# Windowed attention and two feed-forward layers on one core: the planner's order, with offsets for twelve stretches in place of three

## The chip, the core and the metric

The kernel runs on one core of a Trainium2 chip. The metric is the device time of one execution in microseconds (us), the median of several runs. Engine names are those of the profile: PE is TensorE, DVE VectorE, ACT ScalarE, POOL GpSimd, SP the engine that only issues transfers; PEld is the loading of PE's weights.

## What is computed

```python
# q, k, v: (4, 8, 576, 64); heads 0-3 see a window of 32 keys, heads 4-7 every 4th key of 128
scores = scale * np.matmul(q, k.transpose(0, 1, 3, 2))
attn = softmax(np.where(masks, scores, -1e9))
x = np.matmul(attn, v)                      # as (2304, 512)
h = x @ w_in                                # (512, 2048)
x = (h * np.cos(h)) @ w_out                 # (2048, 512)
gate = 1.0 / (1.0 + np.exp(-(x @ w_gate)))  # (512, 1536)
out = (gate * (x @ w_val)) @ w_out2         # (1536, 512)
```

## The kernel before, in words

The 2304 tokens are cut into 6 chunks of 384. Every matrix product of the two layers is made of three PE products, because each operand is split into a high and a low part (`mm3`, lines 896 to 898: high by low, low by high, high by high).

**Attention.** It runs in 24 pairs (12 groups of 192 tokens, plain and dilated heads), two groups to a chunk. For each pair there is `load_qk` (lines 619 and 626), `load_v` (685, 689, 696), a transpose on PE (`transp`, 705), copies out of it (`q_out` and `k_out`, 723 and 727), `scores` on PE (740), the maximum on DVE (`s_max`, 752), the exponential on ACT (`s_exp`, 759), `s_eps` and `s_rec` on DVE (762, 765), `s_norm` on POOL (769), another transpose (`p_transp`, 774), a copy (`p_out`), the product with v (`pv`, 793), and the split of the result into `x_hi` (ACT, 810) and `x_u` or `x` (DVE, 814).

**First layer.** It has 96 steps (chunk and block of 128 hidden columns): all six chunks with blocks 0 to 7, then all six with blocks 8 to 15. Step n has 12 products `h` into one of two PSUM banks `ps_h`, then a chain that alternates ACT and DVE: `turn` (946), `part` (950), `cos` (953), `g` (956, it frees the bank), `g_hi` (963, or on DVE 961), `g_lo` (966). Its end allows the 12 products `x2` into `acc`. The attention of the next chunks is woven between the steps.

**Weights.** They come from memory as 512 KB pieces. Each goes through `w_load` (SP, lines 480 and 483, two buffers `raw`), `w_low` and `w_mag` (ACT, 487 and 492), `w_shift` and `w_rnd` (DVE, 496 and 503; `w_rnd` gives the `raw` buffer back, so the load after the next one can start), `w_hi` (ACT 510 or DVE 508) and the low part `w` (POOL, 514). The weights of the second layer are prepared while the first one runs: sums of blocks on DVE (`w_sum`, 564), high parts on ACT (`w_bhi`, 572), low parts `w_blo` (576; the function `lo` of `block_tasks` takes the engine as an argument), then a transfer to memory (`w2_save`, 581). There are 18 such blocks of four low parts each; blocks 12 to 17 belong to the last product.

**Second layer.** Three sections (pairs of chunks) of 12 steps with 42 products (1203 to 1205), each followed by sums on DVE (1221, 1232), sigmoids on ACT (1229, 1236) and products on DVE (1239); between them and behind them the products with the last weights (`o`, 1351 to 1353, whose operands `o_hi` and `o_lo` make, 1326 and 1330), fed by loads `ow` (1337).

**What sets the order.** No engine chooses at run time. Class `Plan` holds every piece of work as a task with an engine, a duration, the tasks it depends on, buffers it takes and gives, and a number `prio`. `Plan.run` (line 112 on) goes through the run in its own reckoning of time; whenever an engine falls free, it takes the ready task with the lowest `prio`. `Plan.emit` then writes each engine's instructions in that order, the transfers of SP too. An engine works through its instructions strictly in this order, so an instruction that has to wait holds up all behind it. The `prio` of a task of the first layer is the number of its step, of a task that feeds one the number of the step that it is for, less a lead; the chain of a step has its number less `URGENT` (20). The second layer starts at 96 and each of its steps adds 2.75. To this `Plan.add` (line 132) adds an offset by kind of task, from one of three tables: `NUDGE` for `prio` under 16, `NUDGE_MID` under 44, `NUDGE_LATE` from there on (20, 23 and 18 entries, none larger than 9.25).

`MOVES` (line 61) is a list that `emit` applies after the planning: the four low parts `w_blo` of block 16 and the four of block 17 are taken out of POOL's order and put into DVE's, ahead of the tasks named.

**Filler.** While `cold()` holds (until step 7 has begun), `keep_warm` (line 1466) lets PE do bfloat16 products on an identity matrix whenever the plan has nothing else for it. Their results are not used.

Of the kernel before, what the change touches and what calls it, by code (L numbers as in the profile page):

```python
# [46 lines left out]
QK_LEAD, V_LEAD = 3.2, 3.6  # L47
A_LEAD, EXP_LEAD = 2.1875, 0.5
COLD, DENSE = 1.25, 1.0
NUDGE_UNTIL, NUDGE_FROM = 16, 44  # L50
NUDGE = {"k_out": -1.25, "load_qk": -0.25, "load_v": 1.25, "p_out": -7, "p_transp": 0.5, "pv": -3.5, "q_out": -1.25,
         "s_eps": 4.75, "s_exp": 1, "s_max": 2, "s_move": -1.25, "s_norm": -8, "scores": -4, "w": -5.75, "w_mag": -2.5,
         "w_rnd": 0.25, "w_top": -2.5, "x_hi": -6, "x_save": -4.5, "x_u": -5}
NUDGE_MID = {"head": -5.5, "k_out": 4, "load_v": -1.5, "p_out": -0.75, "p_transp": -4.25, "pv": -2.25, "q_out": -2.5,
             "s_eps": 5, "s_exp": -4.25, "s_max": -5.5, "s_norm": 1.5, "s_rec": -5, "scores": -2.25, "transp": -5.25, "w_hi": 3.25,
             "w_load": -1, "w_mag": 7.5, "w_rnd": 2.25, "w_shift": 1, "w_top": 4.25, "x": 0.5, "x_hi": -4.75, "x_u": 5.25}
NUDGE_LATE = {"o_lo": -5.75, "o_sum": 6, "ow": 3, "w2": -4.75, "w2_save": 1.75, "w_blo": -0.5, "w_load": 2.25,
              "w_low": -2.5, "w_mag": 1, "w_rnd": 0.5, "w_sum": 2.5, "w_top": 3.5, "x2_load": -2.25, "x2_take": -0.25, "x_again":
              5.75, "xs": 9.25, "xs_hi": 5.5, "xs_sum": -2}
MOVES = [(("w_blo", 16, 0), "dve", ("g", 92)), (("w_blo", 16, 1), "dve", ("g", 92)), (("w_blo", 16, 2), "dve",  # L60
         ("part", 93)), (("w_blo", 16, 3), "dve", ("part", 93)), (("w_blo", 17, 0), "dve", ("x2_take", 11, 0)), (("w_blo", 17,
         1), "dve", ("x2_take", 11, 0)), (("w_blo", 17, 2), "dve", ("x2_take", 11, 0)), (("w_blo", 17, 3), "dve", ("x2_take",
         11, 0))]
WARM, WARM_NS = 1200, 57


class Plan:
# [28 lines left out]
    def add(self, key, eng, dur, fn, deps=(), prio=0.0, take=(), give=(), table=None, port=False, lat=None, step=None,  # L96
            after=(), gate=None, alt=None, other=None, dma=0):
        assert key not in self.tasks, key
        if key[0] != "warm":
            prio += (NUDGE if prio < NUDGE_UNTIL else NUDGE_MID if prio < NUDGE_FROM else NUDGE_LATE).get(key[0], 0.0)  # L100
        self.tasks[key] = dict(key=key, eng=eng, dur=dur, fn=fn, deps=deps, prio=prio, take=take, give=give, table=table,
                               port=port, lat=lat or 0, step=step, after=after, gate=gate, alt=alt, other=other, dma=dma)

# [135 lines left out]
    def emit(self, todo):  # L239

        at = {k: i for i, (k, e, fn) in enumerate(todo)}
        eng = {k: e for k, e, fn in todo}
        queue = {e: [k for k, x, fn in todo if x == e] for e in ("pe", "act", "dve", "pool", "sp")}
        for k, e, ahead in MOVES:
            queue[eng[k]].remove(k)
            eng[k] = e
            queue[e].insert(queue[e].index(ahead), k)
        count, then, free = {}, {}, dict(self.room)
        for k, t in self.tasks.items():
            ds = set(t["deps"]) | set(t["after"])  # L250
            count[k] = len(ds)
            for d in ds:
                then.setdefault(d, []).append(k)
        for q in queue.values():
            for a, b in zip(q, q[1:]):
                then.setdefault(a, []).append(b)
                count[b] += 1
        self.progress = None
        ready, held = [at[k] for k in at if not count[k]], []
        heapq.heapify(ready)  # L260
        left = len(todo)
        while ready:
            i = heapq.heappop(ready)
            k, e, fn = todo[i]
            t = self.tasks[k]
            if any(free[g] < t["take"].count(g) for g in t["take"]):
                held.append(i)
                continue
            if eng[k] != e:
                fn = t["fn"] if eng[k] == t["eng"] else (t["alt"] or t["other"])[2]  # L270
            for g in t["take"]:
                free[g] -= 1
            if t["step"] is not None:
                self.progress = t["step"]
# [12 lines left out]
        assert not left, "the moves leave no order"
# [3 lines left out]
def windowed_attention_mlp_kernel(ctx, tc, q, k, v, w_in, w_out, w_gate, w_val, w_out2, out):  # L291
# [164 lines left out]
    def w_tasks(i):  # L456
# [63 lines left out]
        else:  # L520
            gate = need - 8 if kind == "out2" else min(W_GATE[2] + j * W_GATE[3], need - 8)
        add(("w_load", i), "sp", 550, load, [], pr - 2 if i >= 2 * FIRST[0] else max(NEG_GS * (i / 4 - 6) + W_START, pos(-A_LEAD - 1) - QK_LEAD + 0.1), take=["raw"], dma=1900, gate=gate,
            after=[("w_load", w_order[w_order.index(i) - 1])] if i else [])
        add(("w_low", i), "act", 520, low, [("w_load", i)], pr)

        def keep():
# [991 lines left out]
```

## Time and profile before

| | |
|---|---|
| time, median of 3 runs | 911.76 us (911.38 to 912.44) |
| span of the profiled execution, first to last instruction | 910.6 us |
| PE busy | 901.8 us, 99% |
| DVE, ACT, POOL busy | 670.4, 502.1, 173.7 us |
| chain that ended last | PE 88%, DMA 5%, ACT 3%, DVE 2% |
| bytes moved | 225.66 MB, 248 GB/s on the mean |

The span is of one execution; the time of a run adds what lies before the first and behind the last instruction. Busy time counts a stretch once in which several products overlap: a 384 column product is listed with some 335 ns, but the next one starts some 171 ns after it (146 of them fill 25 us). "idle before" of a group is the time in which its engine stood still just before it, with what ended that.

### The profile page before, as it was taken

To read this page: it belongs to the slowest core of one execution; us is meant where nothing else is said; L and a number is where in the kernel's file an instruction comes from. 1 tells how busy PE (TensorE), PEld (TensorE's weight loads), DVE (VectorE), ACT (ScalarE), POOL (GpSimd) and SP (SyncE) were. 2 spreads that over 40 slices of the span, in tenths; PEclk is the share of its full clock that TensorE was granted. 3 is DMA by queue.
4 is the path that set the end of the run, shared out by engine and by line. 5 is a ranking of instruction groups with operands and counts; after the bars stand their busy time and mean duration, and the time that the engine had idled before them with its cause. 6 is when DMAs were issued, how large, how long until landed. Compare 5 with 4: busy or idle time off the path is not lost.

```text
span 910.6 us, 19170 instructions
## 1 busy us (share of the span) xinstructions
PE 901.8 (99%) x6898; PEld 883.8 (97%) x6898; DVE 670.4 (74%) x1656; ACT 502.1 (55%) x1216; POOL 173.7 (19%) x200
## 2 busy tenths in 40 slices
PE   8999999999999999999999999999999999999998
PEld 7899999999999999999999999999999999999998
DVE  6987878877768978757899665786566776566583
ACT  5898889878867656655667312252333343332261
POOL 4535232222236443331230000000000000000000
PEclk9999999999999999999999999999999999999999
DMA  8976856754366899975987798877888997887593
GB/s 205 256 209 200 241 150 207 234 166 129 114 205 259 295 371 340 313 248 181 342 252 287 248 345 269 297 244 250 265 275 274 325 304 242 268 268 216 191 329 98
DMA packets 153039, 225.66 MB, mean 248 GB/s; under 512 B 41968, under 2 KB 117488, under 8 KB 151920
## 3 DMA queue, kind: packets, MB, share of 16 engines
q1 hardware_dynamic: 152144, 224.24, 76.1%
q8 instruction: 55, 0.90, 0.4%
q14 instruction: 40, 0.33, 0.1%
q10 hardware_dynamic: 800, 0.20, 0.1%
HBM read 168.82 MB, written 55.57 MB: 246 GB/s over the span
## 4 chain that ended last, share of the span: by engine, by line
PE 88%; DMA 5%; ACT 3%; DVE 2%; issue 1%; POOL 1%; SPq 0%; POOLq 0%; ACTq 0%; DVEq 0%
PE ps_h L896 7%; PE acc L896 7%; PE acc L898 7%; PE acc L897 7%; PE ps_h L898 7%; PE ps_h L897 7%; PE ps_y L1203 4%; PE ps_y L1204 4%; PE ps_y L1205 4%; PE xy L1351 3%; PE xy L1353 3%; PE xy L1352 3%; PE ps_x L1203 3%; PE ps_x L1205 3%; PE ps_x L1204 3%; PE ps_z L1203 2%
## 5 line engine op out<-in xcount | busy, mean ns | idle before, releaser
L576 POOL TENSOR_TENSOR lr<-lf,lr 128x512 fp32r<-128x512 f32 x64 | 82.1, 1299 | 137.6 <-ACT lr L572 135.9
L896 PE MATMUL acc<-gs,arena 128*128 128x384 f32 x240 | 83.3, 347 | 0.0
L898 PE MATMUL acc<-gs,arena 128*128 128x384 f32 x240 | 80.6, 336 | 0.0
L897 PE MATMUL acc<-gs,arena 128*128 128x384 f32 x240 | 80.4, 335 | 0.0
L946 ACT ACTIVATE r<-ps_h 128x384 int32<-128x384 f32 x96 | 46.9, 488 | 50.2 <-PE ps_h L898 50.0
L1203 PE MATMUL ps_y<-arena 128*128 128x384 f32 x216 | 72.9, 338 | 0.6 <-DVE u L1221 0.3
L1205 PE MATMUL ps_y<-arena 128*128 128x384 f32 x216 | 72.3, 335 | 0.0
L1204 PE MATMUL ps_y<-arena 128*128 128x384 f32 x216 | 72.3, 335 | 0.0
L896 PE MATMUL ps_h<-arena 128*128 128x384 f32 x192 | 68.4, 356 | 1.7 <-DVE arena L814 1.6
L956 DVE TENSOR_TENSOR u<-ps_h,u 128x384 f32<-128x384 f32 x96 | 52.8, 553 | 22.5 <-ACT u L953 22.1
L966 DVE TENSOR_TENSOR gs<-u,gs 128x384 fp32r<-128x384 f32 x96 | 60.9, 634 | 11.3 <-ACT gs L963 10.9
L950 DVE SCALAR_TENSOR_TENSOR u<-ps_h,r 128x384 f32<-128x384 f32 x96 | 52.9, 551 | 19.5 <-ACT r L946 18.8
L953 ACT ACTIVATE u<-u 128x384 f32<-128x384 f32 x96 | 49.8, 522 | 30.2 <-DVE u L950 29.5
L1236 ACT ACTIVATE sg<-sg 128x384 f32<-128x384 f32 x36 | 18.9, 526 | 85.4 <-DVE sg L1232 85.4
L898 PE MATMUL ps_h<-arena 128*128 128x384 f32 x192 | 64.6, 336 | 0.0
L898 PE MATMUL ps_h<-arena,wb 128*128 128x384 f32 x192 | 64.6, 336 | 0.0
L897 PE MATMUL ps_h<-arena,wb 128*128 128x384 f32 x192 | 64.5, 336 | 0.0
L896 PE MATMUL ps_h<-arena,wb 128*128 128x384 f32 x192 | 64.5, 336 | 0.0
L897 PE MATMUL ps_h<-arena 128*128 128x384 f32 x192 | 64.4, 336 | 0.0
L759 ACT ACTIVATE s<-s,mx 128x80 f32<-128x80 f32 (+1 forms) x168 | 59.2, 356 | 0.1
L1326 ACT ACTIVATE arena<-ub 128x384 fp32r<-128x384 f32 x62 | 30.9, 520 | 38.0 <-PE xy L1353 26.0
L492 ACT ACTIVATE wc<-wst 128x512 f32<-128x512 f32 x68 | 45.0, 663 | 7.5 <-DMA wst<-in_moe_w_in_dram 3.3
(225 smaller groups left out, 2887.7 us busy)
## 6 DMA issues: line engine op xcount, KB each, us to landing
arena<-wd SPq DMA_DIRECT2D x108, 512.0 KB, 4.7
lr<-od SPq DMA_DIRECT2D x42, 512.0 KB, 4.7
wd<-lr SPq DMA_DIRECT2D x36, 512.0 KB, 5.0
wst<-in_moe_w_out_dram SPq DMA_DIRECT2D x28, 512.0 KB, 5.3
arena<-od SPq DMA_DIRECT2D x21, 512.0 KB, 6.0
arena<-wd SPq DMA_DIRECT2D x36, 256.0 KB, 3.9
od<-lr SPq DMA_DIRECT2D x18, 512.0 KB, 4.7
wst<-in_moe_w_in_dram SPq DMA_DIRECT2D x16, 512.0 KB, 4.8
```

The source lines that it names most:

```text
L576: on.tensor_tensor(out=l, in0=x, in1=h.bitcast(F32), op=ALU.subtract)
L759: ACT.activation(out=s, in_=s, func=AF.Exp, scale=-1.0, bias=row("mx", u)[:, i:i + 1], accum_out=row("rs", u)[:, i:i + 1])
L896: PE.matmul(ps, wh, xl, start=first, stop=False)
L897: PE.matmul(ps, wl, xh, start=False, stop=False)
L898: PE.matmul(ps, wh, xh, start=False, stop=last)
L950: DVE.scalar_tensor_tensor(st["u"], st["h"], INV_2PI, st["r"], op0=ALU.mult, op1=ALU.subtract)
L953: ACT.activation(out=st["u"], in_=st["u"], func=AF.Sin, scale=TWO_PI, bias=HALF_PI)
L956: DVE.tensor_tensor(out=st["u"], in0=st["h"], in1=st["u"], op=ALU.mult)
L966: DVE.tensor_tensor(out=st["gs"][:, 1, :], in0=st["u"], in1=st["gs"][:, 0, :].bitcast(F32), op=ALU.subtract)
L1203: PE.matmul(st[to], wh, xl, start=first, stop=False, **more)
L1204: PE.matmul(st[to], wl, xh, start=False, stop=False, **more)
L1205: PE.matmul(st[to], wh, xh, start=False, stop=kk == 1, **more)
```

## The change

The three tables become one, `NUDGES`, of twelve tables with 289 entries. A task takes the first whose bound lies above its `prio`: 4, 9, 16, 30, 44, 60, 80, 96, 116, 140, 165, or no bound. The values run from -53 to 90.75, and many more kinds have one, the chain of a step among them (`turn`, `part`, `cos`, `g`, `g_hi`, `g_lo`). Because the chain's `prio` is 20 under its step, the first table holds for the chains of steps 0 to 23, the fourth for steps 36 to 49. `MOVES` is gone, and with it the two places in `emit` that applied it, so all 72 low parts `w_blo` are on POOL. No task is added or taken away, no size, buffer or transfer changes. Nine of the twelve tables are cut here.

```diff
-NUDGE_UNTIL, NUDGE_FROM = 16, 44
-NUDGE = {"k_out": -1.25, "load_qk": -0.25, "load_v": 1.25, "p_out": -7, "p_transp": 0.5, "pv": -3.5, "q_out": -1.25,
-         "s_eps": 4.75, "s_exp": 1, "s_max": 2, "s_move": -1.25, "s_norm": -8, "scores": -4, "w": -5.75, "w_mag": -2.5,
-         "w_rnd": 0.25, "w_top": -2.5, "x_hi": -6, "x_save": -4.5, "x_u": -5}
...
-MOVES = [(("w_blo", 16, 0), "dve", ("g", 92)), (("w_blo", 16, 1), "dve", ("g", 92)), (("w_blo", 16, 2), "dve",
-         ("part", 93)), (("w_blo", 16, 3), "dve", ("part", 93)), (("w_blo", 17, 0), "dve", ("x2_take", 11, 0)), (("w_blo", 17,
-         1), "dve", ("x2_take", 11, 0)), (("w_blo", 17, 2), "dve", ("x2_take", 11, 0)), (("w_blo", 17, 3), "dve", ("x2_take",
-         11, 0))]
+NUDGE_UNTIL = 16
+NUDGES = (
+    (4, {"cos": 11, "g": 2.5, "g_hi": 14.5, "g_lo": -14.5, "head": -7.5, "k_out": -0.75, "load_qk": -0.25,
+         "load_v": 30.75, "p_out": -2.75, "p_transp": -1.75, "part": 2.5, "pv": -1.5, "s_eps": 42.5,
+         "s_exp": 1.25, "s_norm": -28, "s_rec": 3, "scores": -2, "transp": 0.25, "turn": -3.5, "w": -1.25,
+         "w_load": 1.5, "w_low": 0.25, "w_mag": -2.5, "w_rnd": 34.5, "w_shift": -0.5, "x": 0.25, "x2": 0.5,
+         "x_hi": -15.75, "x_save": -4}),
...
+    (30, {"cos": 41, "g": 18.5, "g_hi": 10.5, "g_lo": -2, "head": 5, "load_qk": 1, "load_v": 0.5,
+          "p_out": -3.75, "p_transp": 2.5, "part": -4, "q_out": -2.75, "s_eps": 9.5, "s_exp": 1, "s_max": 15,
+          "s_norm": -4.5, "s_rec": -2.25, "scores": -53, "transp": -0.5, "turn": 2.5, "w_keep": 8.75,
+          "w_load": -5, "w_low": -10.5, "w_mag": -6.75, "x2": -0.5, "x2_save": 1.25, "x2_take": -2.75,
+          "x_hi": 2, "x_save": -5.75, "x_u": -8.75}),
...
+    (96, {"gate_b": -1.5, "h": -45.25, "keep": 1.5, "mul": 1.75, "sig_a": -6, "sig_b": 9, "u2": -17.5,
+          "u3": -3, "va": 6.75, "vb": 21, "w2": 1, "w2_save": 0.5, "w_again": -4.75, "w_bhi": -4.75,
+          "w_blo": 10, "w_load": 2.25, "w_low": 1.75, "w_mag": 4.5, "w_rnd": 37.5, "w_sum": 32, "x2": 2.75,
+          "x2_load": 0.25, "x2_save": -9, "x2_take": -6, "x_again": 5, "xs": 9.25, "xs_hi": -9,
+          "xs_load": -0.5, "xs_sum": 12.25}),
...
+)
@@
-            prio += (NUDGE if prio < NUDGE_UNTIL else NUDGE_MID if prio < NUDGE_FROM else NUDGE_LATE).get(key[0], 0.0)
+            prio += next(d for end, d in NUDGES if prio < end).get(key[0], 0.0)
@@
-        for k, e, ahead in MOVES:
-            queue[eng[k]].remove(k)
-            eng[k] = e
-            queue[e].insert(queue[e].index(ahead), k)
@@
-            if eng[k] != e:
-                fn = t["fn"] if eng[k] == t["eng"] else (t["alt"] or t["other"])[2]
```

## Rows read from the trace of the kernel before

**Rows 1.** The page, busy time, share of the span and instructions of each engine:

```profile
PE 901.8 (99%) x6898; PEld 883.8 (97%) x6898; DVE 670.4 (74%) x1656; ACT 502.1 (55%) x1216; POOL 173.7 (19%) x200
```

**Rows 2.** Busy time of PE by stretch of the span (PEclk: granted clock):

```profile
core 0: us, PE busy (x), PEclk, DMA share, GB/s
0.00:100.00 100.00, 95.23 (x1220) 1.00 0.82 217
100.00:250.00 150.00, 149.64 (x1550) 1.00 0.59 175
250.00:525.00 275.00, 275.00 (x1586) 1.00 0.80 279
525.00:605.00 80.00, 79.43 (x471) 1.00 0.86 293
605.00:870.00 265.00, 265.00 (x1771) 1.00 0.81 262
870.00:911.00 41.00, 37.45 (x310) 1.00 0.61 196
```

**Rows 3.** The last product of all, PE in order of time:

```profile
907.21 0.28 PE L1353 MATMUL zz<-arena 128*128 128x256 f32 x1
```

**Rows 4.** The filler of line 1466 alone, by stretch: PE, PEld, clock, DMA:

```profile
0.00:4.60 4.60, 2.97 (x28) 2.91 (x28) 1.00 0.56 126
4.60:33.00 28.40, 11.53 (x161) 10.14 (x159) 1.00 1.00 232
33.00:54.00 21.00, 2.68 (x36) 2.24 (x36) 1.00 0.99 268
54.00:75.00 21.00, 1.34 (x21) 1.24 (x21) 1.00 0.62 170
```

**Rows 5.** The page's groups, first and third product of a set of three:

```profile
L896 PE MATMUL acc<-gs,arena 128*128 128x384 f32 x240 | 83.3, 347 | 0.0
L898 PE MATMUL acc<-gs,arena 128*128 128x384 f32 x240 | 80.6, 336 | 0.0
...
L896 PE MATMUL ps_h<-arena 128*128 128x384 f32 x192 | 68.4, 356 | 1.7 <-DVE arena L814 1.6
...
L898 PE MATMUL ps_h<-arena 128*128 128x384 f32 x192 | 64.6, 336 | 0.0
```

**Rows 6.** PE in order of time: the first product of a step:

```profile
32.98 0.44 PE L896 MATMUL ps_h<-arena 128*128 128x384 f32 x1 [0.42 <-DVE arena L814]
```

**Rows 7.** The same stretches, all engines: PE, PEld, DVE, ACT, POOL, clock, DMA:

```profile
4.60:33.00 28.40, 26.54 (x463) 23.85 (x461) 22.49 (x118) 21.21 (x83) 12.14 (x20) 1.00 1.00 232
33.00:54.00 21.00, 19.79 (x229) 18.38 (x230) 18.46 (x66) 17.91 (x54) 10.29 (x15) 1.00 0.99 268
```

**Rows 8.** Line 896 alone, one of its groups: min/median/max ns, first and last start:

```profile
L896 PE MATMUL acc<-gs,arena x240: 334/334/445, 53.3 to 511.3; 128*128 128x384 f32 x120
```

**Rows 9.** The low parts of line 576, by engine: min/median/max ns, first and last start:

```profile
L576 POOL TENSOR_TENSOR lr<-lf,lr x64: 725/1300/1842, 261.6 to 480.5; 128x512 fp32r<-128x512 f32 x48, 128x256 fp32r<-128x256 f32 x16
L576 DVE TENSOR_TENSOR lr<-lf,lr x8: 415/682/689, 488.3 to 508.5; 128x512 fp32r<-128x512 f32 x6, 128x256 fp32r<-128x256 f32 x2
```

**Rows 10.** Block 17 in order of time: high parts (ACT), low parts (DVE):

```profile
499.88 0.62 ACT L572 ACTIVATE lr<-lf 128x512 fp32r<-128x512 f32 x1
...
503.18 0.42 ACT L572 ACTIVATE lr<-lf 128x256 fp32r<-128x256 f32 x1
...
506.73 2.22 DVE L576 TENSOR_TENSOR lr<-lf,lr 128x512 fp32r<-128x512 f32 x4
```

**Rows 11.** All engines around blocks 16 and 17 (columns as in rows 7):

```profile
475.00:500.00 25.00, 25.00 (x146) 25.00 (x145) 23.52 (x52) 16.90 (x37) 2.00 (x2) 1.00 0.78 290
500.00:525.00 25.00, 25.00 (x146) 25.00 (x145) 15.42 (x31) 8.28 (x15) 0.00 (x0) 1.00 0.75 251
```

**Rows 12.** Two like DVE subtractions, beside POOL's work and after it: min/median/max ns:

```profile
L966 DVE TENSOR_TENSOR gs<-u,gs x96: 543/557/1594, 47.0 to 506.3; 128x384 fp32r<-128x384 f32 x96
...
L1330 DVE TENSOR_TENSOR arena<-ub,arena x62: 544/550/561, 534.0 to 896.2; 128x384 fp32r<-128x384 f32 x62
```

**Rows 13.** SP's waits between 0 and 80 us (us in total, times, longest):

```profile
SPq L483 <- DVE wc L503: 7.6, 4, 3.6
...
SPq L480 <- DVE wc L503: 3.9, 3, 2.6
```

**Rows 14.** DVE, groups of one tile shape: ns of a copy out of a transpose:

```profile
L727 DVE COPY pt<-psa 96x384 f32<-96x384 f32 x16 | 8.4, 546 | 1.6 <-PE psa L774 1.4
```

More of the change, by code (lines that the diff above doesn't have):

```diff
@@ L49 @@
 COLD, DENSE = 1.25, 1.0
-NUDGE_UNTIL, NUDGE_FROM = 16, 44
-NUDGE = {"k_out": -1.25, "load_qk": -0.25, "load_v": 1.25, "p_out": -7, "p_transp": 0.5, "pv": -3.5, "q_out": -1.25,
-         "s_eps": 4.75, "s_exp": 1, "s_max": 2, "s_move": -1.25, "s_norm": -8, "scores": -4, "w": -5.75, "w_mag": -2.5,
-         "w_rnd": 0.25, "w_top": -2.5, "x_hi": -6, "x_save": -4.5, "x_u": -5}
-NUDGE_MID = {"head": -5.5, "k_out": 4, "load_v": -1.5, "p_out": -0.75, "p_transp": -4.25, "pv": -2.25, "q_out": -2.5,
-             "s_eps": 5, "s_exp": -4.25, "s_max": -5.5, "s_norm": 1.5, "s_rec": -5, "scores": -2.25, "transp": -5.25, "w_hi": 3.25,
-             "w_load": -1, "w_mag": 7.5, "w_rnd": 2.25, "w_shift": 1, "w_top": 4.25, "x": 0.5, "x_hi": -4.75, "x_u": 5.25}
@@ L57 @@
-NUDGE_LATE = {"o_lo": -5.75, "o_sum": 6, "ow": 3, "w2": -4.75, "w2_save": 1.75, "w_blo": -0.5, "w_load": 2.25,
-              "w_low": -2.5, "w_mag": 1, "w_rnd": 0.5, "w_sum": 2.5, "w_top": 3.5, "x2_load": -2.25, "x2_take": -0.25, "x_again":
-              5.75, "xs": 9.25, "xs_hi": 5.5, "xs_sum": -2}
-MOVES = [(("w_blo", 16, 0), "dve", ("g", 92)), (("w_blo", 16, 1), "dve", ("g", 92)), (("w_blo", 16, 2), "dve",
-         ("part", 93)), (("w_blo", 16, 3), "dve", ("part", 93)), (("w_blo", 17, 0), "dve", ("x2_take", 11, 0)), (("w_blo", 17,
-         1), "dve", ("x2_take", 11, 0)), (("w_blo", 17, 2), "dve", ("x2_take", 11, 0)), (("w_blo", 17, 3), "dve", ("x2_take",
-         11, 0))]
+NUDGE_UNTIL = 16
@@ new lines @@
+NUDGES = (
[4 more added lines that the diff above has]
+         "x_hi": -15.75, "x_save": -4}),
+    (9, {"cos": -15.25, "g": 5.25, "g_hi": -9, "g_lo": 2, "head": 4.75, "k_out": -4.75, "load_qk": -4.75,
+         "load_v": -11, "p_out": -5.5, "p_transp": -2, "part": 0.25, "pv": -25, "q_out": -3.25,
+         "s_eps": -10.75, "s_exp": 0.75, "s_norm": 8.25, "s_rec": -1, "scores": -5.25, "transp": -4.75,
+         "turn": -7.5, "x2": -0.75, "x_hi": -1.25}),
+    (16, {"cos": -12, "g": 0.5, "g_hi": -4, "g_lo": -2.75, "h": 0.75, "head": -4.25, "k_out": 4, "load_qk": 1,
+          "load_v": 2, "p_transp": -24.75, "q_out": 1, "s_eps": 5.5, "s_exp": -10.5, "s_max": -2, "s_norm": -7,
+          "s_rec": 2, "scores": -0.75, "transp": -2, "turn": -2.75, "x2_save": -7, "x2_take": -2,
+          "x_hi": -21.5, "x_save": -7, "x_u": -11.5}),
+    (30, {"cos": 41, "g": 18.5, "g_hi": 10.5, "g_lo": -2, "head": 5, "load_qk": 1, "load_v": 0.5,
[3 more added lines that the diff above has]
+          "x_hi": 2, "x_save": -5.75, "x_u": -8.75}),
+    (44, {"g": 3.25, "g_lo": 17.5, "head": -3.75, "k_out": 6.75, "load_qk": -11.5, "load_v": -0.5, "p_out": -1,
+          "p_transp": 15.75, "part": 8.75, "pv": -6, "s_eps": 0.5, "s_exp": 0.5, "s_max": -4.5, "s_norm": 7.25,
+          "s_rec": 7.75, "scores": 5.5, "transp": 5.25, "turn": 3.75, "w": 6, "w_hi": -4, "w_load": -10.5,
+          "w_low": -2.5, "w_mag": -4.5, "w_rnd": -12.5, "w_shift": 1.5, "x": 0.25, "x2": 90.75, "x_hi": -8}),
+    (60, {"cos": -6.25, "g": -22.75, "g_lo": -0.25, "part": 20.75, "turn": 5.25, "w": 7, "w_hi": 18.5,
+          "w_load": -3.25, "w_low": 18.25, "w_mag": -8.25, "w_rnd": 0.25, "w_shift": 1.5, "x2": 0.25,
+          "x2_save": 4.5}),
+    (80, {"cos": 3, "g": 6, "g_hi": 8.25, "g_lo": -24, "gate_b": 8, "h": -0.25, "keep": 1.5, "mul": -6.75,
+          "part": 3, "sig_a": 17.25, "sig_b": -1.5, "turn": 6.75, "u2": 7, "u3": -2, "va": -9.75,
+          "w2_save": -4.75, "w_bhi": 15, "w_blo": -19.75, "w_load": -6, "w_rnd": -7.75, "w_shift": -24.5,
+          "w_sum": 0.5, "x2_load": 9.75, "x2_save": -1, "x2_take": 3}),
+    (96, {"gate_b": -1.5, "h": -45.25, "keep": 1.5, "mul": 1.75, "sig_a": -6, "sig_b": 9, "u2": -17.5,
[3 more added lines that the diff above has]
+          "xs_load": -0.5, "xs_sum": 12.25}),
+    (116, {"gate_b": -12.75, "keep": 6, "o_sum": -5.25, "p": -8.75, "sig_a": 2, "u2": 10.5, "u3": 4, "vb": -2,
+           "w2": 2, "w_again": 4, "w_bhi": -6.25, "w_blo": 2.75, "w_load": -3.25, "w_low": 7.75, "w_mag": 3.5,
+           "w_rnd": -2, "w_sum": -15, "x2_save": 6, "x2_take": -4.75, "xw_load": 1.25, "xw_sum": 7}),
+    (140, {"gate_b": 2.75, "keep": 5, "o": 3, "o_A0": 5, "o_hi": -2, "o_keep": -3, "o_lo": -17.25,
+           "o_save": 19.25, "o_sum": -0.5, "o_u2": -27.5, "ow": 7, "sig_a": -4.5, "sig_b": 2.75, "u2": -4,
+           "u3": -14.5, "va": 1, "vb": -17.25, "w2": 2, "w_bhi": 3, "w_load": 9.5, "w_low": 25.25, "w_rnd": 1,
+           "w_shift": 1.25, "w_sum": 33.5, "xs": 11, "xs_hi": 1}),
+    (165, {"gate_b": -1, "keep": -18.5, "mul": 3, "o": -7, "o_A1": 14.25, "o_B0": 5.25, "o_B1": -4.75,
+           "o_hi": 9, "o_lo": 0.25, "o_save": -11.75, "o_sum": -7.5, "o_u3": -24.25, "ow": -8.75, "p": -8,
+           "sig_a": -9, "sig_b": 7, "u2": 5.5, "u3": 11.5, "va": 1, "vb": -16.5, "w2": 38, "xs": 31.5,
+           "xs_hi": 11, "xw_load": 0.75, "xw_sum": -0.75}),
+    (float("inf"), {"gate_b": 1, "keep": 2, "mul": -19.25, "o": -0.75, "o_A0": -5, "o_B0": 5.5, "o_B1": -4,
+                    "o_hi": -8.25, "o_lo": 18.5, "o_save": 2.75, "o_sum": 18, "o_u2": 17.75, "p": -6,
+                    "sig_a": 4.5, "sig_b": 3, "va": 7.5, "w2": 4.5}),
+)
```

## The prediction

> **What bounds the kernel now.** I read the busy times first. PE is busy for 901.8 of 910.6 us and no other engine comes near it [rows 1]. A busy PE may still do nothing of use, so the second question is where it stands idle or does filler. The stretches answer the first half: between 250 and 525 us, and again between 605 and 870 us, PE is busy in every microsecond (275.00 of 275.00, 265.00 of 265.00), between 525 and 605 us it loses 0.57 us, between 100 and 250 us 0.36 us [rows 2]. What is idle lies in the first 100 us (100 less 95.23 = 4.8 us) and in the end, where 910.6 less the start of the last product at 907.21 is 3.4 us of copying and storing [rows 2, 3]. The filler answers the second half: 2.97 + 11.53 + 2.68 + 1.34 = 18.5 us, all before 75 us [rows 4]. The third loss is inside the busy time. The first product of a set that follows other work is listed longer than its neighbours: 347 against 336 ns in one group and 356 against 336 in another, so (11 x 240 + 20 x 192) ns = 6.5 us over the run go into restarting PE after a turn to attention or after a wait [rows 5].
>
> So everything that an order can give back is some 4.8 + 18.5 us in the start, 6.5 us in turns, and about 1 us behind that. The rest is products, which the change does not touch. Wherever PE is full now, an earlier or later job of DVE, ACT, POOL or SP costs nothing until it makes PE wait. The granted clock is 1.00 in each stretch, which is the level of 2.4 GHz; nothing is to be gained there [rows 2].
>
> **The change, part by part.** The sum is made against the span of 910.6 us; the median run of 911.8 us lies 1.2 us above it, and I carry these 1.2 us along.
>
> *The start (the first three tables).* Of the 23.3 us lost, the stretch up to 4.6 us waits for the first loads and the identity matrix; its 1.63 us of idle (4.60 less 2.97) and 2.97 us of filler are out of reach, since no reordering makes bytes land sooner than the first one asked for [rows 4]. Up to 33 us there is no product of a step, because the first one waits for the split of the attention result of chunk 0 (0.42 us before it at 32.98) [rows 6]. In these 28.4 us PE has 11.53 us of filler and 1.9 us of idle, DVE has 5.9 us free and ACT 7.2 us [rows 4, 7]. From 33 to 54 us filler and idle are 2.68 + 1.2 us, with DVE at 18.46 and ACT at 17.91 of 21 us [rows 4, 7]. The table for `prio` under 4 now says: exponentials' sums (`s_eps`) and rounding of weights (`w_rnd`) behind everything else on DVE, `load_v` behind the weights on SP, `x_hi` and `s_norm` first. That favours the copies and maxima which feed PE, and that is the way in which the first step could come earlier. If all of DVE's 5.9 us were put to use, the first step would come 5.9 us earlier, and the 3.9 us up to 54 us might go as well: 9.8 us is the upper bound. The lower bound is a loss (the second rival). What limits it is the row on transfers: the DMA share is 1.00 and 0.99 up to 54 us [rows 4], so no byte is moved sooner unless another is moved later. I take 3 us, half of DVE's free time before the first step, nearer to the full queues than to the free engine. **-3.0 us.**
>
> *Turns (tables three to five).* Scores, transposes and products with v are ranked anew against `h` and `x2`; `scores` at -53 goes first whenever it is ready. If attention's pieces come in larger groups, PE turns less often. At 6.5 us in all and some 110 ns for one, 445 against 334 ns at the most [rows 8], there are about 60 turns; saving one in eight gives 0.8 us. The bounds are 2 us either way, a third of the rows' sum. **-0.8 us.**
>
> *The late stretches (tables six to twelve).* PE loses 0.57 us from 525 to 605 us and nothing up to 870 us [rows 2]. Whatever else is moved there, `w_sum` by +32, `w_rnd` by +37.5, `u2`, `vb` and the `o` tasks, is covered by the two `ps_h` banks: a bank is free again long before PE is back at it. If that cover went, each wait would cost its length and a restart. I take half of what is lost, bounded by 0.6 us of gain and 2 us of loss. **-0.3 us.**
>
> *The eight low parts.* On DVE they take 6 x 682 + 2 x 415 ns = 4.9 us at the most; on POOL eight take 6 x 1300 + 2 x 725 ns = 9.3 us [rows 9]. On the path lies block 17, the last one, since its `w2_save` and the load `ow` behind it stand ahead of the first `o` products on SP. Its high parts are done on ACT between 500.5 and 503.6 us, but DVE comes to the low parts only at 506.73 and ends at 508.95 [rows 10]. POOL, which does nothing from 482 us on [rows 9, 11], could start at 500.5 and need 3 x 1300 + 725 ns = 4.6 us, so it would be done at about 505.1, earlier than DVE. Block 16 is made and saved ahead of block 17 either way and is not on this path. DVE gets 4.9 us back in a stretch where it is busy for 23.52 + 15.42 of 50 us, and PE waits for nothing there [rows 11]. **0 us**, with bounds of 0.5 us either way.
>
> There is something that speaks against it. DVE's subtraction at line 966, made while POOL works, takes 557 ns in the median but up to 1594; the same shape at line 1330, after POOL's last instruction, never exceeds 561 [rows 12]. So POOL's work holds DVE up now and then. The Trainium skill, page "SBUF — State Buffer", section "SBUF: two separate sides", says why: VectorE and GpSimd share one pair of ports, and whichever starts first keeps it for its whole instruction while the other is blocked. The trace agrees in kind. By that rule alone the eight parts hold DVE for up to 9.3 us.
>
> By the rows, DVE gives up 4.9 us and may be held for 9.3, a net 4.4 us at the worst, against 1.5 + 9.6 us that it has free in these two stretches; so the term stays at 0 [rows 11].
>
> Sum: 911.8 - 3.0 - 0.8 - 0.3 + 0 = **907.7 us**.
>
> **The rivals.**
> *It only changes places.* In the start the transfers set the pace: share 1.00 and 0.99 up to 54 us [rows 4]. Then a different rank of the same jobs moves filler from one stretch to another, and the rest of the run is full anyway [rows 2]. Offsets also do nothing where only one job is ready. For it: the DMA share, and DVE and ACT at 85 to 88% after 33 us. Against it: 11.5 us of filler before 33 us with both engines free for a fifth of it [rows 4, 7]. Time: 911.8 less the turns' 0.8, 911 us. That includes the case that the change does not do what it says.
>
> *Weights come late (slower).* Place: `w_rnd` on DVE in the first 75 us. It is what gives the `raw` buffer back, and SP's loads of weights already wait for it seven times, for 7.6 + 3.9 = 11.5 us [rows 13]. With +34.5 it stands behind every other ready job on DVE. Behind a waiting load on SP stand the loads of q, k and v, and behind a late weight `h` and `x2`. One job more in front of each rounding is 546 ns [rows 14]; twelve of the sixteen first weights are loaded after the first four, so 12 x 0.55 = 6.6 us. It decides from the point at which a weight of the first eight steps lands later than PE gets to it: after 54 us there is only 1.34 us of filler to absorb that [rows 4]. Time: 911.8 + 6.6 - 1.3 = 917 us. For it: a DVE with 88% busy rarely gets to its last job. Against it: 2.5 us of 21 are still free there [rows 7], and a rank behind only counts while something else is ready.
>
> *DVE held by POOL, or a bank late (slower).* The chain of steps 36 to 49 has `cos` at +41, behind all other work of ACT, and the eight parts hold DVE. Each would need to use up the slack of a bank. If three or four steps lost 1 us each, 915 us. For it speaks only the maximum of 1594 ns [rows 12]; against it that PE lost 0.36 us in 150 with the same cover [rows 2].
>
> **How the numbers follow.** A measurement of this kernel tells 0.2% (1.8 us) from no change. Forecast (start and turns give 2 to 10 us): 0.58. Changes places: 0.18. Weights late: 0.16, DVE held or a bank late: 0.08. So faster 0.58, same 0.18, slower 0.24. The range reaches from most of the start's bound, 911.8 - 9.8 = 902, to just under the price of late weights, 916.5: outside lie a tenth below and a tenth above. The likeliest case alone is 903 to 910.
>
> **What would show it.** Right: fewer than 244 fillers, the last before 71 us; the first step product before 33 us, by about the gain; line 576 on POOL alone, 72 times, with block 17 saved no later than now; no new PE wait after 250 us. Weights late: the waits of lines 480 and 483 for line 503 grow past 11.5 us, and filler grows between 33 and 75 us. DVE held: line 966 or 950 with a longer mean, and PE waits between 200 and 525 us. The forecast is wrong if the filler stays near 18.5 us and the time still moves by over 2 us, for then the gain or loss came from a place I call full.

## The result, and the profile after

The changed kernel takes 917.49 us in the median of six runs (915.92 to 918.55), the kernel before 911.57 us in six runs beside them. The ratio is 1.0051, with a 95% interval from 1.0036 to 1.0066: slower by 0.5%, about 4.7 us. Ratio and interval are taken over all of these runs, so the ratio need not be the quotient of the two medians. The prediction of 907.7 us had the wrong sign, and the result lies above its range. The profiled execution has a span of 915.2 us (before 910.6) and a run time 1.8 us above that.

In the changed kernel every source line below the tables stands 31 lines further down: line 927 is line 896 of before, 997 is 966, 607 is 576. The page's busy times, against [rows 1]:

```profile
PE 902.5 (99%) x6877; PEld 883.7 (97%) x6877; DVE 668.3 (73%) x1632; ACT 510.5 (56%) x1234; POOL 183.4 (20%) x208
```

The engines do nearly the work that they did: POOL has 9.7 us more, for its eight parts, ACT 8.4 us more, DVE 2.1 us less. The loss is in waits, and busy time by stretch, set against [rows 2], says where (PE busy, then granted clock, DMA share and GB/s):

```profile
0.00:100.00 100.00, 94.72 (x1178) 1.00 0.85 222
...
200.00:250.00 50.00, 48.98 (x509) 1.00 0.47 137
250.00:450.00 200.00, 197.58 (x1185) 1.00 0.78 277
450.00:525.00 75.00, 75.00 (x432) 1.00 0.79 278
525.00:605.00 80.00, 79.56 (x472) 1.00 0.83 280
605.00:870.00 265.00, 264.56 (x1752) 1.00 0.80 260
```

From 250 to 450 us, where PE had been busy without a gap, it now stands idle for 2.42 us, from 200 to 250 us for 1.02 us and from 605 to 870 us for 0.44 us. Between 200 and 870 us that makes 4.32 us idle, where the kernel before has the 0.57 us of 525 to 605 us and no more. Each stop adds a restart of some 0.1 us that counts as busy [rows 8]. With the 3.75 us of idle time that are new, that is most of the 4.6 us by which the span grew. The first 100 us are no better than before: 5.28 us idle in place of 4.77.

PE's waits between 200 and 300 us, and between 440 and 450 us, name what came late (us in total, times, longest):

```profile
PE ps_h L927 <- DVE u L987: 1.5, 2, 1.0
PE acc L927 <- DVE o L1061: 0.2, 1, 0.2
...
PE acc L927 <- DVE gs L997: 1.6, 1, 1.6
```

The longest one is the easiest to follow. First DVE, then POOL, then PE in order of time:

```profile
440.70 0.42 DVE L527 TENSOR_SCALAR wc<-wc 128x512 int32<-128x512 int32 x1
441.04 0.35 DVE L992 CAST gs<-u 128x384 fp32r<-128x384 f32 x1
441.31 1.52 DVE L595 TENSOR_TENSOR lf<-lf 128x256 f32<-128x256 f32 x1
442.75 1.61 DVE L997 TENSOR_TENSOR gs<-u,gs 128x384 fp32r<-128x384 f32 x1
444.28 0.68 DVE L534 CUSTOM_DVE_ANT_0 lf<-wst,wc 128x1024 uint16<-128x1024 uint16 x1
...
441.12 2.82 POOL L607 TENSOR_TENSOR lr<-lf,lr 128x512 fp32r<-128x512 f32 x2 [5.18 <-ACT lr L603]
...
444.41 0.44 PE L927 MATMUL acc<-gs,arena 128*128 128x384 f32 x1 [1.61 <-DVE gs L997]
```

The sum on line 595 takes 1.52 us where its median is 0.42, and the subtraction `g_lo(78)` on line 997 takes 1.61 us where its median is 0.56, while POOL's two low parts of block 13 run beside them for 2.82 us. PE has finished `x2(77)` and stands still until `g_lo(78)` is there. In the kernel before, `g_lo(78)` came right behind `g(79)` on DVE. In the new order eight jobs stand between them: the shift and the rounding of weight 59, three sums of block 13, the shift of weight 60, `g_hi(78)`, which was on ACT, and `w_sum(13,3)`. What was there 4.9 us early in the old order (the rows are below, where the prediction is answered) is now late when POOL holds DVE: the two holds make up (1.52 - 0.42) + (1.61 - 0.56) = 2.2 us, the wait is 1.6 us.

In the same way `h(43)` waits at 280.95 us for 0.46 us, behind a shift of 1.52 us and a `g_lo` of 1.19 us, and `x2(40,3)` waits at 287.69 us for 0.23 us behind a cast of 1.42 us and a sum of 1.50 us. The wait at 219.28 us has another cause: `cos(30)` stands on ACT behind `w_mag(25)`, whose weight was late from memory. ACT in order of time:

```profile
217.56 0.66 ACT L523 ACTIVATE wc<-wst 128x512 f32<-128x512 f32 x1 [2.09 <-DMA wst<-in_moe_w_in_dram]
218.13 0.51 ACT L984 ACTIVATE u<-u 128x384 f32<-128x384 f32 x1
```

### The profile page after: what moved, and what is told of

Its sections match the earlier page's. It is cut to its first block, busy times and chain, and to the rows that moved or that the text cites. A ratio compares the mean times of both kernels' runs of the same rounds, so it can differ in the third digit from the quotient of the medians.

```text
span 915.2 us, 19166 instructions
## 1 busy us (share of the span) xinstructions
PE 902.5 (99%) x6877; PEld 883.7 (97%) x6877; DVE 668.3 (73%) x1632; ACT 510.5 (56%) x1234; POOL 183.4 (20%) x208
## 4 chain that ended last, share of the span: by engine, by line
PE 50%; DVE 1%; DMA 1%; SPq 0%; issue 0%; ACT 0%; DVEq 0%
PE ps_y L1234 4%; PE ps_y L1236 4%; PE ps_y L1235 4%; PE xy L1382 3%; PE xy L1384 3%; PE xy L1383 3%; PE ps_x L1234 3%; PE ps_x L1236 3%; PE ps_x L1235 3%; PE ps_z L1234 3%; PE ps_z L1235 3%; PE ps_z L1236 3%; PE zz L1382 1%; PE zz L1384 1%; PE zz L1383 1%; PE acc L927 1%
## 5 line engine op out<-in xcount | busy, mean ns | idle before, releaser
L607 POOL TENSOR_TENSOR lr<-lf,lr 128x512 fp32r<-128x512 f32 (+1 forms) x72 | 91.7, 1293 | 139.5 <-ACT lr L603 112.1
L997 DVE TENSOR_TENSOR gs<-u,gs 128x384 fp32r<-128x384 f32 x96 | 64.2, 670 | 15.1 <-ACT gs L994 14.2
```

Of the source, the lines that this page charges most:

```text
L607: on.tensor_tensor(out=l, in0=x, in1=h.bitcast(F32), op=ALU.subtract)
L997: DVE.tensor_tensor(out=st["gs"][:, 1, :], in0=st["u"], in1=st["gs"][:, 0, :].bitcast(F32), op=ALU.subtract)
```

## The experiments

An edit of the form `(job, engine, next)` puts that job ahead of the job `next` on that engine; where `MOVES` is added to the changed kernel, the two places in `emit` that apply it are back too (not printed). "Ratio" is to the kernel before on the same chip, with its 95% interval.

**The eight parts alone.** The kernel before without its moves, so that only the low parts of blocks 16 and 17 go to GpSimd:

```diff
-MOVES = [(("w_blo", 16, 0), "dve", ("g", 92)), (("w_blo", 16, 1), "dve", ("g", 92)), (("w_blo", 16, 2), "dve",
...
```

> The kernel before with the eight low parts of blocks 16 and 17 back on POOL and nothing else changed. Theory (the loss of the changed kernel comes from a few places between 200 and 450 us where the new order puts a step's chain behind work that is held up): no change, 911.6 us within 0.6, and no new PE wait between 480 and 530 us. Rival (the eight parts themselves cost it, by holding DVE or by a later save of block 17): 914.5 us or more, with a PE wait behind 488 us.

Measured: 914.17 us, ratio 1.0022 (1.0014 to 1.0031), 2.0 us slower. PE has a new wait, and the trace shows the hold in front of it (waits, DVE, POOL):

```profile
PE ps_y L1193 <- DVE u L946: 1.3, 1, 1.3
...
501.90 1.66 DVE L1077 TENSOR_TENSOR arena<-xt,arena 128x384 fp32r<-128x384 f32 x1
503.48 1.43 DVE L951 CAST gs<-u 128x384 fp32r<-128x384 f32 x1
504.83 0.54 DVE L946 TENSOR_TENSOR u<-ps_h,u 128x384 f32<-128x384 f32 x1
...
501.77 4.27 POOL L566 TENSOR_TENSOR lr<-lf,lr 128x512 fp32r<-128x512 f32 x3 [7.29 <-ACT lr L562]
```

Three of block 17's parts hold a subtraction and a cast, and `g(95)` comes 1.3 us late. So the theory written before this run, no change, was wrong: the parts are not free in the old order.

**The start alone.** The changed kernel with its first three tables, the old ones behind them (written here by their old names) and the old moves:

```diff
-    (30, {"cos": 41, "g": 18.5, "g_hi": 10.5, "g_lo": -2, "head": 5, "load_qk": 1, "load_v": 0.5,
...
+    (44, NUDGE_MID),
+    (float("inf"), NUDGE_LATE),
 )
+MOVES = [(("w_blo", 16, 0), "dve", ("g", 92)), (("w_blo", 16, 1), "dve", ("g", 92)), (("w_blo", 16, 2), "dve",
...
```

> The first three of the new tables (prio under 16), then the old middle and late tables and the old list of moves. Theory: the start is a wash, 911.6 us within 1.2; PE has done as much useful work by 200 us as before. Rival (late weights in the first 75 us, a loss that is carried on): 914 us or more, filler over 18.5 us. My forecast on record would have it at 908.6.

Measured: 913.11 us, ratio 1.0001 (0.9991 to 1.0012). In its profile the first product of a step starts at 32.22 us, 0.76 us before [rows 6], and the filler is 14.20 + 2.53 = 16.7 us in place of 18.5 [rows 4]. The time does not show it: the start is worth nothing that can be measured.

**The later tables alone.** The changed kernel with the old first table, up to `prio` 16 and written here by its old name, in the place of its first three; the eight parts stay on GpSimd:

```diff
 NUDGES = (
-    (4, {"cos": 11, "g": 2.5, "g_hi": 14.5, "g_lo": -14.5, "head": -7.5, "k_out": -0.75, "load_qk": -0.25,
...
+    (16, NUDGE),
     (30, {"cos": 41, "g": 18.5, "g_hi": 10.5, "g_lo": -2, "head": 5, "load_qk": 1, "load_v": 0.5,
```

> The old first table up to prio 16, then the nine new tables from there on; no moves. Theory: the loss is made by these tables, so 914 to 918 us, with PE waits of 0.4 to 2 us in a few places between 200 and 450 us (not at the same steps, since the start is another one). Rival (late weights in the start): 912.5 us or less.

Measured: 920.55 us, ratio 1.0090 (1.0076 to 1.0104). The same wait for a `g_lo` (1.6 us) stands in its profile, and three for a `g` (2.7 us in all, the longest 1.8 us near 304 us). The tables from `prio` 16 on make the loss by themselves. They lose more than the whole change does and more than was expected, so the parts of the change do not simply add up.

**No GpSimd at 442 us.** The two low parts that run there go to VectorE, behind `g_lo(78)`:

```diff
+MOVES = [(("w_blo", 13, 0), "dve", ("w_rnd", 60)), (("w_blo", 13, 1), "dve", ("w_rnd", 60))]
```

> The changed kernel with two low parts of block 13 put on DVE behind the last piece (g_lo) of step 78's chain, so that POOL does nothing while DVE makes the sum and g_lo at 441 to 444 us. DVE's order in front of g_lo stays. Theory (POOL holds DVE: the sum took 1.52 us in place of 0.42 and g_lo 1.61 in place of 0.55): the sum and g_lo take 0.42 and 0.55 us, PE's wait of 1.61 us before the x2 products of step 78 goes, span 1.7 us (1.3 to 2.1) under 915.2. Rival (g_lo is simply too far back in DVE's order): the wait stays over 1 us and the span within 0.6 of 915.2.

Measured: 916.5 us, ratio 1.0042 (1.0028 to 1.0055). With POOL silent the sum and `g_lo(78)` have their usual length again, and PE's wait of 1.61 us is gone. But the edit carries its own cost, 1.28 us of DVE ahead of `part(80)`, and PE then waits 0.76 us for `g(80)`, which frees the bank of the next `h`. The profiled span is 915.1 us, so the 1.7 us did not come back (DVE in order of time, then PE's waits):

```profile
441.87 0.42 DVE L605 TENSOR_TENSOR lf<-lf 128x256 f32<-128x256 f32 x1
442.20 0.55 DVE L1007 TENSOR_TENSOR gs<-u,gs 128x384 fp32r<-128x384 f32 x1
442.68 1.28 DVE L617 TENSOR_TENSOR lr<-lf,lr 128x512 fp32r<-128x512 f32 x2
...
PE ps_h L937 <- DVE u L997: 0.8, 1, 0.8
```

**`cos(30)` ahead of the late weight.**

```diff
+MOVES = [(("cos", 30), "act", ("w_mag", 25))]
```

> The kernel after, with one job moved on ACT: cos(30) stands ahead of w_mag(25), whose load came late at 217 us. Theory (the in-order queue of ACT makes cos(30) and so h(32) late): PE's wait of 1.02 us at 219 us is gone, its restart too, and nothing else waits in its place, so 917.5 - 1.2 = 916.3 us. Rival (the weight itself is late for its own step, and the wait only moves on): PE waits about 1 us a little later, time 917.5 us.

Measured: 915.63 us, ratio 1.0033 (1.0020 to 1.0046). `w_mag(25)` still waits 1.9 us for its weight, but behind `cos(30)`, and PE's wait of 1.02 us at 219 us is gone. One of 0.39 us stands at 220 us in its place: a transpose waits for a copy on ACT behind the same late weight. The interval does not part this run from the changed kernel; the trace shows that the wait for `g(30)` comes from ACT's queue.

**`w_sum` behind `g_lo`.** The order of two DVE jobs, POOL left as it is:

```diff
+MOVES = [(("w_sum", 13, 3), "dve", ("w_rnd", 60))]
```

> The kernel after, with one job moved on DVE: w_sum(13,3) stands behind g_lo(78), not ahead of it. GpSimd's two low parts of block 13 stay where they are. Theory (GpSimd's instruction at 441.1 us holds whichever DVE instruction comes next until it ends): g_lo(78) (line 997) now takes 1.2 to 1.6 us in the place of w_sum, ends near 442.8 us, and PE's wait of 1.61 us falls to 0.3 to 0.6. Rival (only the order of the queue counts, and the long durations are not held by GpSimd): g_lo(78) takes 0.55 us, ends near 441.9 us and PE does not wait at all. Time by either 917.5 less 1.1 to 1.7, 916.1 us; it is the row of line 997 that tells them apart.

Measured: 917.49 us, ratio 1.0047 (1.0028 to 1.0065), no gain. Its row of `g_lo(78)` is what the theory expected, and the sum behind it is held as well:

```profile
441.57 1.53 DVE L1006 TENSOR_TENSOR gs<-u,gs 128x384 fp32r<-128x384 f32 x1
443.02 1.50 DVE L604 TENSOR_TENSOR lf<-lf 128x256 f32<-128x256 f32 x1
444.45 0.68 DVE L543 CUSTOM_DVE_ANT_0 lf<-wst,wc 128x1024 uint16<-128x1024 uint16 x1
```

So it is not the job that is long, it is whatever stands there. PE waits 0.2 us for `g_lo(78)` and then 1.3 us for `g(80)`, which now comes late. Neither theory had the second wait.

**Four places at once.**

```diff
+MOVES = [(("cos", 30), "act", ("w_mag", 25)), (("w_sum", 13, 3), "dve", ("w_rnd", 60)),
+         (("w_shift", 34), "dve", ("g_lo", 40)), (("g_lo", 40), "dve", ("x2_take", 4, 1)),
+         (("x2_take", 4, 3), "dve", ("w_sum", 0, 3)), (("w_sum", 0, 3), "dve", ("part", 43))]
```

> The kernel after, with six jobs moved in four places and everything else left: cos(30) ahead of w_mag(25) on ACT (219 us); on DVE w_sum(13,3) behind g_lo(78) (444 us), w_shift(34) and part(41) in turn and g_lo(40) behind g(41) (281 us), x2_take(4,3) ahead of w_sum(0,3) (288 us). Theory (the loss is four or five chains that the new order puts behind a held or late job): 1.2 + 1.3 + 0.5 + 1.0 = 4.0 us back, 913.5 us. Rival (the loss is spread over the new order, and each place repaired leaves another one late): 916 us or more, with new PE waits behind these.

Measured: 917.79 us, ratio 1.0044 (1.0029 to 1.0059). By the time the rival was right. The profiled execution took 913.98 us, 3.8 less than the median, so it does not show all of the loss. In it the waits at 219, 281 and 288 us are gone, but a new one of about 1.6 us stands at 300 us, where POOL's low parts hold another cast, sum and `g_lo` (1.46, 1.51 and 1.07 us), and the one at 444 us is as in the run above. Moving jobs of DVE under POOL's holds moves the wait.

**The eight parts back on VectorE, in the new order.**

```diff
+MOVES = [(("w_blo", 16, 0), "dve", ("g", 92)), (("w_blo", 16, 1), "dve", ("g", 92)), (("w_blo", 16, 2), "dve",
...
```

> The kernel after, with the eight low parts of blocks 16 and 17 on DVE again, ahead of the same jobs as in the kernel before. Theory (the loss lies in the new order between 200 and 450 us; what the eight parts cost depends on where a hold meets a chain, and in the new order PE loses only 0.5 us between 450 and 525 us): 917.5 - 0.5 = 917.0 us. Rival (the eight parts carry 2 us of the loss, as they did alone in the old order): 915.5 us. Second rival (the new order has no room for them on DVE): 918.5 us or more, with a PE wait near 500 us.

Measured: 924.42 us, ratio 1.0131 (1.0111 to 1.0151), far off on the slow side. SP's queue has the saves of block 17 ahead of the load that `x2_take(11,2)` needs, in this order as in the old one. But the place named for the parts comes later here: DVE ends them at 513.79 us, not at 508.95 [rows 10]. One save waits 12.2 us, the load behind it is late, and DVE stands 6.17 us waiting for it:

```profile
SPq L622 <- DVE lr L617: 14.2, 4, 12.2
...
529.78 0.56 DVE L1067 TENSOR_TENSOR lf<-acc,lf 128x384 f32<-128x384 f32 x1 [6.17 <-DMA lf<-x2h]
```

It is no measure of what the parts cost in the new order. It shows that their place on DVE and the orders of DVE and SP around it belong together.

**GpSimd's low parts cut short, in both orders.** Queues and semaphores stay; POOL leaves most of each low part uncomputed, so its time in it falls (cut here: ACT fills in those of block 0, four more instructions):

```diff
...
+            c = slice(0, 16) if on is POOL else slice(None)
-            on.tensor_tensor(out=l, in0=x, in1=h.bitcast(F32), op=ALU.subtract)
+            on.tensor_tensor(out=l[:, c], in0=x[:, c], in1=h[:, c].bitcast(F32), op=ALU.subtract)
```

In the changed kernel:

> The kernel after, with GpSimd's 72 low parts of the blocks cut to 16 columns of each row (the rest is left uncomputed, so the output is not the reference's; block 0's are filled in by ACT, four instructions of some 0.6 us). Order, queues and semaphores stay; what goes is the time in which GpSimd's instruction can hold DVE. Theory (in the new order these holds stand ahead of chains that PE waits for at 281, 288, 444 and 526 us): w_sum and g_lo near 444 us take 0.42 and 0.55 us in the place of 1.52 and 1.61, PE's wait of 1.61 us there and the one at 288 us go, the one at 219 us stays; 917.5 - 3.0 = 914.5 us. Rival (it is the order of DVE's own work that makes the chains late, holds or not): the waits stay within 0.3 us, 917 us.

In the kernel before:

> The same cut in the kernel before (64 low parts on GpSimd; the eight on DVE stay whole). Theory: there no hold stands ahead of a chain that PE waits for, so the time stays as it is, -0.5 to 0 us against before, and the distance between the two orders falls from 4.6 us to 1.5 to 2.5. Rival (order alone): the distance stays 4.6 us. If GpSimd's holds cost both orders the same, this one falls by 3 us too.

Measured: 913.83 us, ratio 1.0013 (1.0004 to 1.0022), for the new order, and 912.16 us, ratio 1.0009 (0.9995 to 1.0023), for the old one. The distance between the orders falls from 0.51% to 0.04%, from 4.7 to about 0.4 us; by the intervals up to some 2 us may be left. The old order gains nothing from the cut. The page of the new order, and PE by two of the stretches as above:

```profile
PE 900.3 (99%) x6877; PEld 882.6 (97%) x6877; DVE 641.7 (70%) x1632; ACT 511.9 (56%) x1238; POOL 112.2 (12%) x208
...
200.00:250.00 50.00, 49.66 (x514) 1.00 0.47 136
250.00:450.00 200.00, 199.79 (x1195) 1.00 0.79 280
```

DVE's busy time falls by 26.6 us though it does the same work: that is time in which POOL's low parts held it. In the old order the same cut takes 670.4 - 648.4 = 22.0 us from it:

```profile
PE 902.2 (99%) x6898; PEld 884.8 (97%) x6898; DVE 648.4 (71%) x1656; ACT 504.4 (55%) x1220; POOL 112.0 (12%) x200
```

So both orders are held for about as long, and only the new one pays for it. (The old order's profiled execution took 914.77 us, 2.6 above the median: PE waits 1.97 us at 577.56 us, for a sum that stands on DVE behind one whose load came late. Behind that the granted clock is 0.81 on the mean up to 580 us and 0.59 up to 583 us, a mix of its two levels, 1.2 and 2.4 GHz. From 200 to 525 us PE is busy throughout.) In the new order, at 439 us, with a POOL instruction of 0.8 us for both parts, the sum and `g_lo(78)` take their usual time, and `g_lo(78)` ends at 439.93 us, 0.67 us before PE reads it (DVE, POOL, PE):

```profile
439.00 0.44 DVE L595 TENSOR_TENSOR lf<-lf 128x256 f32<-128x256 f32 x1
439.36 0.57 DVE L1000 TENSOR_TENSOR gs<-u,gs 128x384 fp32r<-128x384 f32 x1
...
438.72 0.80 POOL L610 TENSOR_TENSOR lr<-lf,lr 128x16 fp32r<-128x16 f32 x2 [8.21 <-DVE wc L527]
...
440.60 0.35 PE L930 MATMUL acc<-gs,arena 128*128 128x384 f32 x1
```

The wait at 219 us is shorter too (0.3 us), although no low part of a block runs there: the weight happened to land earlier. Of the difference between these two profiled executions about 0.7 us is therefore not the holds'; the ratios are over all runs.

**Two waits of the kernel before.** A try at a faster version, on the old order and then with the start tables of the change:

```diff
...
+         (("u3", 8), "dve", ("xw_sum", 1, 0, "s1")), (("u2", 11), "dve", ("xs", 1, 0, "a1")),
```

> The kernel before, with two jobs moved ahead on DVE: u3(8) ahead of the two sums xw_sum(1,0,s1) and xw_sum(1,1,s1), and u2(11) ahead of xs(1,0,a1). Theory (a wait of PE in a full stretch costs its length and a restart): the waits at 575.8, 578.4, 582 and 597.6 us go, 0.9 to 1.2 us, 0.999 of before. Rival (the two sums feed DMA stores or products that are then late): 1.000 or above.

> The three start tables of the change with the old tables behind them and the eight parts on DVE (as in e2), and the two moves of the run above. Theory: the start tables are worth nothing and the moves 1 us, so the same time as the run above, 0.999 of before. Rival (start and moves add up because the start tables help by some 1 us): 0.998.

Measured: 912.9 us, ratio 1.0004 (0.9993 to 1.0015), and 913.14 us, ratio 1.0008 (0.9997 to 1.0018). Neither gains: near 575 us PE's wait for `sg` (0.2 us) gives way to one for `vb` of 0.4 us. No kernel here is faster than the one before.

## Why the prediction was wrong

**The start, -3.0 us: about 0.** The step that failed is "I take 3 us, half of DVE's free time before the first step". In the changed kernel the filler did fall, as the text asked, to 2.97 + 11.60 + 2.68 = 17.2 us in place of 18.5 [rows 4]:

```profile
0.00:4.60 4.60, 2.97 (x28) 2.91 (x28) 1.00 0.60 139
4.60:35.00 30.40, 11.60 (x161) 10.20 (x159) 1.00 0.96 221
35.00:56.00 21.00, 2.68 (x36) 2.23 (x36) 1.00 0.95 259
...
35.07 0.44 PE L927 MATMUL ps_h<-arena 128*128 128x384 f32 x1 [0.49 <-DVE arena L845]
```

But the first product of a step came at 35.07 us, not before 32.98 [rows 6]: less filler is not an earlier step. One execution does not place it well: in the nine profiled ones with the new start tables it comes between 32.22 and 35.07 us, in the five with the old ones between 32.51 and 34.15, so no gain shows. With the start tables by themselves the measured ratio is 1.0001. Two signs named for a right forecast came true all the same, 223 fillers in place of 244 and the last of them at 47.2 us, and they were worth no time. The row that I priced at half, the DMA share of 1.00 and 0.99, was the one that fits, and of the cases the one named "It only changes places" describes this stretch. That the transfers are the reason was not tested.

**Turns, -0.8 us: -0.3.** The page's first products of a set have means of 349 and 352 ns, the third ones 336; by the same working (13 x 240 + 16 x 192) ns = 6.2 us in place of 6.5 [rows 5]. The sign is right and the size small. But the term priced tables three to five by PE's turns alone. They also rank the chains of steps 29 to 63, and that it put at nothing. The jobs that came late at 219, 281 and 288 us, `cos(30)`, `g(41)` and `x2_take(4,3)`, have their offsets from them (the jobs that stood in front partly from later tables), and PE waited 1.02 + 0.46 + 0.23 = 1.7 us there.

**The late stretches, -0.3 us: about +4 (with the waits just named).** The step that failed is that whatever is moved there "is covered by the two `ps_h` banks: a bank is free again long before PE is back at it". That is true of the order before, and I carried it over to an order that spends it. A view of busy time shows that PE waits for nothing; it does not show by how much each job is early, nor how much of that a move takes. In the kernel before, where the plan emits `g_lo` and `x2` step by step, `g_lo(78)` is the 79th run of line 966. It ends at 435.98 us, and PE's first product that reads it starts at 440.83: 4.9 us to spare. Even `g_lo(79)`, which is held beside two of POOL's low parts for 1.40 us, ends at 441.09 us and is not read before 445.02 (DVE, POOL, PE, of the kernel before):

```profile
435.42 0.56 DVE L966 TENSOR_TENSOR gs<-u,gs 128x384 fp32r<-128x384 f32 x1 [0.42 <-ACT gs L963]
435.98 0.43 DVE L496 TENSOR_SCALAR wc<-wc 128x512 int32<-128x512 int32 x1
...
439.69 1.40 DVE L966 TENSOR_TENSOR gs<-u,gs 128x384 fp32r<-128x384 f32 x1
...
439.38 2.86 POOL L576 TENSOR_TENSOR lr<-lf,lr 128x512 fp32r<-128x512 f32 x2 [4.78 <-ACT lr L572]
...
440.83 0.35 PE L896 MATMUL acc<-gs,arena 128*128 128x384 f32 x1
...
445.02 0.35 PE L896 MATMUL acc<-gs,arena 128*128 128x384 f32 x1
```

Over steps 36 to 87 of that kernel no `x2` starts less than 2.5 us behind the end of its `g_lo`, and no `h` less than 1.1 us behind the `g` that frees its bank. In the changed kernel the least is under 0.1 us for both. At `x2(78)` the eight jobs ahead of `g_lo(78)` on DVE used up all but half a microsecond of the 4.9 (2.2 us of holds became a wait of 1.6 us; with the low parts cut short 0.67 us are left), and the holds took the rest and more. And the cover that I named belongs to `h`; the products `x2` read `gs`, which no `ps_h` bank covers.

**The eight parts, 0 us: +2.0 by themselves.** The step that failed is the comparison of "a net 4.4 us at the worst, against 1.5 + 9.6 us that it has free in these two stretches". It weighs sums over 25 us, while a hold is paid where it stands ahead of a chain: one hold of block 17's three parts cost PE 1.3 us. Nor was block 17 done by 505.1 us: in the old order POOL ran from 501.77 to 508.33 us. In the new order its last sum on DVE started at 504.63 us, ACT's high parts at 504.03 us, and POOL ran from 504.72 us for 5.02 us, to 509.74 us, later than DVE had been [rows 10]. The 2.0 us are of the old order and do not add to the rest: in the new one PE is busy for all of 450 to 525 us.

Of the sentence from the Trainium skill, page "SBUF — State Buffer", section "SBUF: two separate sides", that an instruction which starts first keeps the shared ports to its end: the runs agree, with 1.52 us for a sum of 0.42 beside POOL, and 0.44 beside a POOL instruction cut to 16 columns. By that rule an instruction of DVE that needs these ports can be late by all that is left of POOL's, and the rows of `g_lo(78)` and of the sum show delays of that size.

**The rivals.** "Weights come late" did not happen in the start: SP's waits for line 534 there are 6.8 + 5.3 = 12.1 us, against 11.5 [rows 13], and the filler behind the first step fell from 4.0 to 2.7 us [rows 4]. "DVE held by POOL, or a bank late", with a chance of 0.08 and 915 us, is what happened. That the holds cost the new order most of its loss, and the old one nothing that can be measured, is shown by the pair of cut kernels. The places are `h(43)`, `x2(40)`, `x2(78)` and the ACT queue at step 30. Two of them lie among the steps that I named, 36 to 49, but what PE waited for there stood behind held jobs of DVE. `cos` on ACT does come late at steps 37 and 38, 3.9 and 2.5 us behind its `part` where it was 0.03 before, and between 220 and 280 us PE has no wait over 0.1 us.

What stays open: the last wait of 0.4 us near 677 us, and why the weight behind the wait at 219 us lands when it does; in the five profiled executions with that part of the order unchanged the wait is between 0.18 and 1.21 us.

## What to carry to other kernels

A stretch without idle time does not say how much slack is in it, and the slack of the old order is not the slack of the new one. Before a reordered queue is priced at nothing, compare when each operand is ready with when it is read. Take from that distance what the new order puts in between, at the length that it has while it is held. Where GpSimd and VectorE work side by side, price a hold by the chain that stands behind it at that moment, not by its sum; and when it does cost, look at GpSimd's instruction first: cutting it short gave the time back here, though at the price of work left out, while moving VectorE's jobs under it changed which of them is late. Moving GpSimd's instruction in time was not tried. Jobs that were moved by hand belong with the queue order made for them, on the DMA queue too.

## What the runs showed of the hardware that was not expected

Not every DVE instruction is held. Between 200 and 515 us of the changed kernel (min/median/max ns):

```profile
L987 DVE TENSOR_TENSOR u<-ps_h,u x69: 542/557/559, 199.7 to 506.8; 128x384 f32<-128x384 f32 x69
L981 DVE SCALAR_TENSOR_TENSOR u<-ps_h,r x68: 540/550/562, 206.2 to 505.0; 128x384 f32<-128x384 f32 x68
...
L997 DVE TENSOR_TENSOR gs<-u,gs x69: 541/558/1643, 205.7 to 512.5; 128x384 fp32r<-128x384 f32 x69
L992 DVE CAST gs<-u x16: 348/356/1449, 204.5 to 470.0; 128x384 fp32r<-128x384 f32 x16
L595 DVE TENSOR_TENSOR lf<-lf x72: 407/418/1519, 277.0 to 504.6; 128x256 f32<-128x256 f32 x72
```

The two that read `ps_h`, which is in PSUM, never exceed 562 ns, and those that read SBUF alone reach 1449 to 1643 ns. The held ones pass it on to the others by standing ahead of them in the queue.

After a wait of 5.76 us in the run with the eight parts on VectorE, PE was granted half of its clock (the 1.2 GHz level) for 6.2 us, and the full 2.4 GHz behind that (its stretches of PE: length, busy, clock, DMA share, GB/s):

```profile
526.00:530.80 4.80, 0.00 (x0) 0.94 1.07 386
530.80:537.00 6.20, 6.14 (x19) 0.50 0.78 304
537.00:545.00 8.00, 8.00 (x47) 1.00 0.71 230
```

Nineteen products take the place of some 36 there, so that one wait cost about 3 us more than its length.
